# w_out converted from 64 to 32 bits during the attention, through a scratch in DRAM

## The chip, the cores and the metric

The kernel runs on one core of one Trainium2 chip. The metric is the device time of one execution in microseconds (us), lower is better. Beside the time there is a profile of one execution, with the start and the duration of each instruction on each engine: TensorE (PE, with its weight loads as PEld), VectorE (DVE), ScalarE (ACT), GpSimd (POOL), and SyncE (SP), which here only issues DMAs.

## The reference

Three stages follow one another. B = 4, H = 8 heads, 512 local and 32 global positions, head size 64, so 2304 tokens of 512 channels.

```python
# 1 attention: global rows see everything, local rows the global ones and a window of 32
out_g = softmax(scale * q_g @ k_all.T) @ v_all
out_l = softmax([scale * q_l @ k_g.T, where(|i - j| <= 32, scale * q_l @ k_l.T, -1e9)]) @ [v_g, v_l]
x = concat([out_g, out_l]).transpose(0, 2, 1, 3).reshape(2304, 512)
# 2 mixture of 8 experts, 288 tokens each, assigned greedily by descending logit
logits = x @ w_gate
for e in range(8):
    out[mask_e] = relu(x[mask_e] @ w1[e]) @ w2[e]         # 512 -> 1024 -> 512
# 3 feed-forward for all tokens
h = out @ w_in                                            # 512 -> 2048
result = (max(h, 0) + log1p(exp(-abs(h)))) @ w_out        # 2048 -> 512
```

The two weights of the third stage, `w_in` (512 x 2048) and `w_out` (2048 x 512), come with 64 bits per number; all other inputs have 32.

## The kernel before

**Numbers.** The products of the experts' stages are made in three passes: each 32-bit operand is split into a high part in the engine's 32-bit matmul format and the rest, and TensorE adds high x high, high x rest and rest x high (`mm3`). A split is one copy (high part, on ScalarE or GpSimd) and one subtraction (rest, on GpSimd through `psub`, or on VectorE). A 64-bit weight must first be made into a 32-bit one, by shifts and masks on its two 32-bit halves.

**Attention** (`attention`, lines 115 to 197) runs in 64 steps of software pipelining, eight to a unit (a pair of batch and half of the heads), and some steps after. A letter of `CFG["order"]` stands for a piece of a step: scores on TensorE (`a`), maximum on VectorE (`m`), exponent on ScalarE (`e`), transposes (`c`), products with V (`d`), normalizing (`n`), logits (`p`), the next unit's K and Q transposes (`u`) and V windows (`v`), the loads of the units to come (`q`, `w`), and the global rows (`g`). Results go to `xs_scratch` in DRAM, the global rows last; these are read back (`xg`) for their logits, the last that the routing waits for (`global_finish`, `lastly`).

**w_in** is converted during the attention. Pieces `k` and `b` call `conv_a(n)` and `conv_b(n)` (lines 260 to 286), for 16 blocks of 128 x 512 numbers. `conv_a` loads a 64-bit block of 512 KB on SP's queue into one of three buffers. `conv_b`, four steps later, takes magnitude and sign (L277 and L278, ScalarE), and a step after that shifts and joins bits (L281, L282, VectorE), multiplies by the sign (L283, which the profile shows as the helper's L255, GpSimd), and stores 256 KB to `win_scratch` (L284, SP's queue). One block goes every three steps, from step 6 on (`"k": 6, "r": 3`). After the attention `load_win` reads the sixteen 32-bit tiles of w_in back, and `conv_win` splits them: copy on ScalarE (L589), subtraction on GpSimd (L258).

**w_out** is loaded as it is, in 64 bits: ten blocks of 512 KB at step 58 (`EARLY`), when the attention's first buffers are given up, and six more after the last store to `xs_scratch`. `conv_wout` (lines 597 to 617) is the conversion in four steps: magnitude on ScalarE (L606), three bit operations on VectorE (L608, L610, L612), then the split, copy on ScalarE (L616) and subtraction on GpSimd (L258).

**After the attention.** `route(0, hop)` finds the tokens of the first expert, by two searches of three levels; at each level VectorE compares (L686, L687), TensorE counts, and VectorE decides. `hop` is called after each comparison but the first and puts steps of `conv_wout` there, by the costs `COST` and the allowance `HOP`. Then the tokens' rows are gathered (`gather`, GpSimd's indirect DMA), transposed and split (`xh`, `xl`). For each expert `moe1` runs the two products of stage 2 over eight blocks `f`, and `moe2` the two of stage 3 over sixteen; the next expert's routing is spread over both. In the first expert `conv` is called with each block and puts there what is left of w_out's steps and the last five of w_in's splits (`NW`, `C0`, `CS`); also, its w1 and w2 blocks are split otherwise than later ones (high part on ScalarE, rest of seven of the w2 blocks on GpSimd).

**Order.** Each engine runs its instructions in its own queue's order. That order is made when the program is built, by a planner that simulates the program's time, with additional edges from `after`, which places the instructions of an engine behind a given instruction of the same engine. DMAs of the kernel are issued on SP's queue, in order, but for the gathers and the final stores (GpSimd).

Of the kernel before, what the change touches and what calls it, by code (L numbers as in the profile page):

```python
# [8 lines left out]
F32 = mybir.dt.float32  # L9
# [10 lines left out]
P = 128  # L20
# [22 lines left out]
CFG = {"order": "adcm*wnpvbehuqkgDxA", "c": 1, "d": 2, "n": 5, "x": 5, "p": 6, "u": 0, "w": 2, "g": [3, 4, 7], "g7": [0, 1, 3], "b": 4, "ps": [1, 2, 2, 3], "pp": 2, "ph": 2, "nb": 2, "xc": 4, "qs": 1, "cv": 3, "k": 6, "r": 3, "m": 0, "e": 0, "h": 1, "z": 4, "uA": 0, "uD": 0, "gD": 0, "gA": 0, "hA": 1, "hD": 1, "nD": 1, "xA": 0, "pD": 1, "cD": 1, "v": [2, 3, 4, 5, 6, 7], "ve": "DPPPPP", "ue": "ADAaaDA", "he": "A", "ge": "DDA"}  # L43
COST = (0.335, 0.6, 0.6, 0.0)
HOP = {64: 1.2, 32: 0.7}
NEARLY = 10
MC = {"MT0": [0, 1, 3, 5, 10, 11, 12, 14, 15, 17, 20, 21, 24, 25, 26], "MT1": [1, 2, 3, 4, 5, 7, 12, 13, 14, 15, 16, 17, 18, 20, 23], "GT": [24, 1], "GW": 10, "AH": 1, "XB": 8, "HEAD": 4, "L2": "bkadc", "lag": {"a": 0, "b": 1, "c": 2, "d": 3}, "bufs": {"sp_e": 3, "sp_u": 3, "gh": 3, "gl": 4, "wh": 4, "wl": 4, "wraw": 4}, "HT0": "ABhhh", "HT1": "Ahhh", "C0": 6, "CS": 0.75, "NW": 11, "NWT": 3, "WH": "PPPA", "WL": "DDDD", "M1L": 2, "H1": 0, "OB": "ADB", "W0": "PPPPPPPD"}
# [8 lines left out]
class K:  # L56
    def __init__(self, tc, ctx, a):
        self.tc = tc
        self.nc = tc.nc
        self.ctx = ctx  # L60
        self.a = a
        self.xs = self.nc.dram_tensor("xs_scratch", (NTOK, D), F32).ap()
        self.wic = self.nc.dram_tensor("win_scratch", (D, DFF), F32).ap()

# [46 lines left out]
    def attention(self):  # L111
# [27 lines left out]
        for s in range(6):  # L139
# [19 lines left out]
            "k": lambda t, u, s, live: (t - G["k"]) % G["r"] == 0 and 0 <= (t - G["k"]) // G["r"] < 16 and self.conv_a((t - G["k"]) // G["r"]),  # L159
            "b": lambda t, u, s, live: (t - G["k"] - G["b"]) % G["r"] == 0 and 0 <= (t - G["k"] - G["b"]) // G["r"] < 16 and self.conv_b((t - G["k"] - G["b"]) // G["r"]),  # L160
# [38 lines left out]
    def half(self, t, fn):  # L199
        if t >= 0 and t % 2 == 0 and t < 64:  # L200
            fn(t // 2)

# [57 lines left out]
    def conv_a(self, n):  # L260
        nc, ap = self.nc, self.ap
        w = 512
        q, cc = n // 4, n % 4
        src = self.a["moe2_w_in"].bitcast(I32)[cc * P:cc * P + P, q * 2 * w:(q + 1) * 2 * w]
        dst = self.wic[cc * P:cc * P + P, q * w:q * w + w]
# [320 lines left out]
    def conv_win(self, f):  # L586
        w = self.wi[f]
        rv = w[:, 1].bitcast(F32)
        self.nc.scalar.copy(w[:, 0], rv)  # L589
        self.psub(w[:, 1], rv, w[:, 0].bitcast(F32))  # L590
# [6 lines left out]
    def conv_wout(self, f):  # L597
        nc, mp = self.nc, self.mp
        rv = self.wo[f].rearrange("p (n t) -> p n t", t=2)
        lo, hi = rv[:, :, 0], rv[:, :, 1]  # L600
        if self.late:
            m, u = (mp.tile([P, D], I32, tag=n, bufs=MC["bufs"][n], name=f"wou{n}{f}") for n in ("wh", "wl"))
        else:
            mu = mp.tile([P, 2, D], I32, tag=("yL", "yh", "yl")[f % 3], bufs=1, name=f"wou{f}")
            m, u = mu[:, 0], mu[:, 1]
        nc.scalar.activation(m.bitcast(F32), hi.bitcast(F32), AF.Abs, scale=2.0 ** -112)  # L606
        yield
        nc.vector.tensor_scalar(u, lo, 29, None, ALU.logical_shift_right)  # L608
        yield
        nc.vector.scalar_tensor_tensor(u, hi, -(2 ** 31), u, ALU.bitwise_and, ALU.bitwise_or)  # L610
        yield
        nc.vector.scalar_tensor_tensor(u, m, 3, u, ALU.logical_shift_left, ALU.bitwise_or)  # L612
        yield
        w = u.bitcast(F32)
        self.wo[f] = o = self.wop.tile([P, 2, D], F32R, tag=f"wo{f}", bufs=1, name=f"wo{f}")
        nc.scalar.copy(o[:, 0], w)  # L616
        self.psub(o[:, 1], w, o[:, 0].bitcast(F32))
# [414 lines left out]
    def moe(self):  # L1032
        self.moe_setup()
# [6 lines left out]
        self.late = False  # L1040
        gens = [self.conv_wout(f) for f in range(16)]
        todo = [(f, i) for f in range(16) for i in range(4)]

        def step():
            f, i = todo.pop(0)
            if i == 0:
                next(gens[f])
            next(gens[f], None)
            return COST[i]
# [11 lines left out]
        with self.after(self.r_ins):  # L1061
            for f in range(MC["NW"]):
                self.conv_win(f)
# [87 lines left out]
```

## Time and profile before

| what | value |
|---|---|
| median of 3 runs | 907.5 us (902.51 to 910.68) |
| the profiled execution | span 906.8 us from its first to its last instruction; no other time is given for it |
| granted TensorE clock, mean | 0.946 |
| busy: PE, PEld | 819.0 us (90%), 717.3 us (79%) |
| busy: DVE, ACT, POOL | 673.6 us (74%), 428.0 us (47%), 453.7 us (50%) |
| DMA | 87.36 MB, mean 96 GB/s |
| chain of waits | PE 64%, DVE 25%, DMA 4%, issue 3%, POOL 2% |

"Busy" is the time in which an engine shows at least one instruction; matmuls are pipelined, so a busy PE need not be at its peak. The chain of waits is followed back from the last instruction, at each step to what released it. The granted clock is the share of full speed that TensorE was given. An instruction carries the line of the kernel that issued it, and a copy or a subtraction through a helper that of the helper (L82 `pcopy`, L255 `pmul`, L258 `psub`). The shares of the whole span are averages over stages with different limits.

### The profile page before, as it was taken

Reading aid. Unit: us, or ns where it says so; the run is one execution under the profiler, and the core shown is the slowest. Engines: PE = TensorE matmul, PEld = TensorE weight load, DVE = VectorE, ACT = ScalarE, POOL = GpSimd, SP = SyncE. Lnnn points to the kernel's source line nnn. Section 1 sums busy time; section 2 is a strip of 40 time slices with the busy share of each in tenths; the row PEclk is TensorE's granted clock in tenths of the full one; section 3 lists DMA queues with packets and bytes.
Section 4 is the critical chain, followed back from the end, with each engine's and each line's share of the span. In section 5 each row is a group of like instructions: output and inputs, shape, how many; then the busy total and the mean of one; then the engine's idle time right before and its main releaser. Section 6 shows DMA issues by size and latency. Waiting matters only on the chain.

```text
span 906.8 us, 20945 instructions
## 1 busy us (share of the span) xinstructions
PE 819.0 (90%) x7608; PEld 717.3 (79%) x7608; DVE 673.6 (74%) x1981; ACT 428.0 (47%) x1067; POOL 453.7 (50%) x608
## 2 busy tenths in 40 slices
PE   7999999931488989999999999999999999999996
PEld 4677767621478869989978998998899899889885
DVE  4776877579999887786795887679588778763632
ACT  3667767532554552453345255244525524442542
POOL 6654758034767554464366265336435643642533
PEclk9999999955588999999999999999999999999999
DMA  6879773792230124122131321303132130312000
GB/s 150 193 208 248 212 202 121 267 311 77 71 94 1 55 64 117 47 72 86 33 94 44 99 70 49 109 10 97 45 95 84 36 117 2 118 59 60 1 1 35
DMA packets 123691, 87.36 MB, mean 96 GB/s; under 512 B 61828, under 2 KB 106884, under 8 KB 123588
## 3 DMA queue, kind: packets, MB, share of 16 engines
q1 hardware_dynamic: 120692, 77.11, 30.0%
q0 software_dynamic: 2896, 8.92, 3.0%
q8 instruction: 60, 0.98, 0.5%
q14 instruction: 43, 0.35, 0.1%
HBM read 72.89 MB, written 13.11 MB: 95 GB/s over the span
## 4 chain that ended last, share of the span: by engine, by line
PE 64%; DVE 25%; DMA 4%; issue 3%; POOL 2%; ACT 1%; SPq 1%; POOLq 0%; ACTq 0%; DVEq 0%
PE accb L1008 12%; PE h L884 8%; PE h L886 8%; PE h L885 8%; PE st L399 4%; PE acca L884 3%; PE acca L885 3%; PE acca L886 3%; DVE sp_e L990 3%; DVE R L811 2%; PE av L447 2%; PE pt L429 2%; DVE gl L999 2%; DVE wl L879 2%; DMA wr<-in_moe_w_dram 1%
## 5 line engine op out<-in xcount | busy, mean ns | idle before, releaser
L1008 PE MATMUL accb<-wo,gh 128*128 128x512 f32 x448 | 131.9, 400 | 1.0 <-ACT gh L998 1.0
L997 POOL TENSOR_TENSOR sp_u<-sp_u,sp_e 128x256 f32<-128x256 f32 x112 | 89.9, 806 | 83.4 <-DVE sp_e L991 33.3
L884 PE MATMUL h<-yh,wi 128*128 128x256 f32 x448 | 127.7, 291 | 0.8 <-DVE yl L943 0.8
L885 PE MATMUL h<-yl,wi 128*128 128x256 f32 x448 | 128.1, 288 | 0.0
L886 PE MATMUL h<-yh,wi 128*128 128x256 f32 x448 | 127.9, 288 | 0.0
L879 DVE TENSOR_TENSOR wl<-wr,wh 128x512 fp32r<-128x512 f32 x121 | 92.5, 778 | 12.8 <-POOL wh L82 9.8
L82 POOL TENSOR_SCALAR wh<-wr 128x512 fp32r<-128x512 f32 x84 | 60.1, 720 | 82.7 <-PE h L885 50.5
L990 DVE SCALAR_TENSOR_TENSOR sp_e<-sp_u,sp_e 128x256 f32<-128x256 f32 x112 | 59.4, 531 | 43.2 <-POOL sp_u L985 43.2
L884 PEld LDWEIGHTS h<-yh,wi 128*128 128x128 f32 x448 | 86.8, 196 | 4.6 <-DVE yl L943 1.0
L886 PEld LDWEIGHTS h<-yh,wi 128*128 128x128 f32 x448 | 87.8, 196 | 3.1
L885 PEld LDWEIGHTS h<-yl,wi 128*128 128x128 f32 x448 | 87.8, 196 | 2.9
L1008 PEld LDWEIGHTS accb<-wo,gh 128*128 128x128 f32 x448 | 77.1, 189 | 12.6 <-ACT gh L998 1.8
L985 POOL TENSOR_SCALAR sp_u<-sp_e 128x256 f32<-128x256 f32 x112 | 64.0, 576 | 44.5 <-ACT sp_e L984 34.0
L886 PE MATMUL h<-xh,wl 128*128 128x272 f32 x256 | 76.4, 299 | 9.2 <-DVE wl L879 9.1
L1008 PE MATMUL accb<-wo,gl 128*128 128x512 f32 x224 | 79.2, 402 | 3.8 <-DVE gl L999 3.7
L992 ACT ACTIVATE sp_u<-sp_u 128x256 f32<-128x256 f32 x112 | 46.7, 417 | 66.8 <-DVE sp_e L990 66.2
L884 PE MATMUL h<-xh,wh 128*128 128x272 f32 x256 | 77.2, 302 | 0.9 <-ACT xh L867 0.9
L885 PE MATMUL h<-xl,wh 128*128 128x272 f32 x256 | 75.4, 295 | 0.0
L885 PE MATMUL acca<-hl,wh 128*128 128x272 f32 x256 | 71.3, 293 | 2.2 <-DVE hl L920 2.2
L919 ACT ACTIVATE hh<-h 128x272 fp32r<-128x272 f32 x64 | 25.4, 396 | 97.7 <-PE h L886 89.3
L886 PE MATMUL acca<-hh,wl 128*128 128x272 f32 x256 | 70.9, 291 | 0.0
L983 ACT ACTIVATE sp_e<-h 128x256 f32<-128x256 f32 (+1 forms) x128 | 49.0, 387 | 43.2 <-PE h L886 43.2
(410 smaller groups left out, 2212.5 us busy)
## 6 DMA issues: line engine op xcount, KB each, us to landing
wr<-in_moe_w_dram SPq DMA_DIRECT2D x128, 256.0 KB, 2.8
wraw<-in_moe_w_in_dram SPq DMA_DIRECT2D x16, 512.0 KB, 5.0
wor<-in_moe_w_out_dram SPq DMA_DIRECT2D x16, 512.0 KB, 7.1
qn<-in_q_l_dram SPq DMA_DIRECT2D x32, 128.0 KB, 2.9
xs_scratch<-xc SPq DMA_DIRECT2D x32, 128.0 KB, 3.9
win_scratch<-cvs SPq DMA_DIRECT2D x16, 256.0 KB, 4.3
wi<-win_scratch SPq DMA_DIRECT2D x16, 256.0 KB, 5.7
kn<-in_k_l_dram SPq DMA_DIRECT2D x40, 96.0 KB, 3.8
```

Of the source, the lines that this page charges most:

```text
L82: self.nc.gpsimd.tensor_scalar(out, in_, 1.0, 1.0, ALU.mult, ALU.mult)
L399: nc.tensor.matmul(o, q[:, pr, i].rearrange("p r q -> p (r q)"), kw, start=True, stop=True)
L879: (nc.gpsimd if (odd and MC["W0"][self.wn // 2 % 8] == "P" if first else MC["WL"][self.wn % 4] == "P") else nc.vector).tensor_tensor(l, ra ...
L884: nc.tensor.matmul(ps, wh, ah, start=start, stop=False)
L885: nc.tensor.matmul(ps, wh, al, start=False, stop=False)
L886: nc.tensor.matmul(ps, wl, ah, start=False, stop=stop)
L983: nc.scalar.activation(e, ps, AF.Abs)
L985: nc.gpsimd.tensor_scalar(u, e, 1.0, 1.0, ALU.add, ALU.mult)
L990: nc.vector.scalar_tensor_tensor(e, u, -1.0, e, ALU.add, ALU.subtract)
L992: nc.scalar.activation(u, u, AF.Ln)
L997: nc.gpsimd.tensor_tensor(u, u, e, ALU.add)
L1008: nc.tensor.matmul(t, g[:, cs], w, start=f == 0 and i == 0, stop=f == 15 and i == 2)
```

## The change

w_out goes the way that w_in goes. `conv_a` and `conv_b` now run for 32 blocks, first 16 of w_out (128 whole rows each, 512 KB in, 256 KB out to the new `wout_scratch`), then the 16 of w_in. They are spread by `spread`: block n at step 1 + floor(15 n / 8), the last at step 59, `conv_b` still four steps later. `load_wout` reads 32-bit blocks of 256 KB, at the same two places. `conv_wout` and `conv_win` go; `split` does a tile's copy (ScalarE) and subtraction (VectorE or GpSimd). The list `todo` has eight w_out tiles, the sixteen of w_in, and the other eight of w_out: `hop` takes two after a comparison with 64 thresholds and one after one with 32, on VectorE; `conv` takes two per block in the first eight blocks of expert 0, the first on GpSimd and the second on VectorE, and then one per block on GpSimd, until none is left. The diff without the tables' unchanged entries and the two `conv_*` functions that go:

```diff
-CFG = {... "k": 6, "r": 3, ...}
-COST = (0.335, 0.6, 0.6, 0.0)
-HOP = {64: 1.2, 32: 0.7}
+CFG = {... "k": 1, "r": 15, ...}
-MC = {... "C0": 6, "CS": 0.75, "NW": 11, "NWT": 3, ...}
+MC = {...}
@@ __init__
+        self.woc = self.nc.dram_tensor("wout_scratch", (DFF, D), F32).ap()
@@ attention
-            "k": lambda t, u, s, live: (t - G["k"]) % G["r"] == 0 and 0 <= (t - G["k"]) // G["r"] < 16 and self.conv_a((t - G["k"]) // G["r"]),
-            "b": lambda t, u, s, live: (t - G["k"] - G["b"]) % G["r"] == 0 and 0 <= (t - G["k"] - G["b"]) // G["r"] < 16 and self.conv_b((t - G["k"] - G["b"]) // G["r"]),
+            "k": lambda t, u, s, live: self.spread(t - G["k"], self.conv_a),
+            "b": lambda t, u, s, live: self.spread(t - G["k"] - G["b"], self.conv_b),
+    def spread(self, t, fn):
+        for n in range(2 * DFF // P):
+            if n * CFG["r"] // 8 == t:
+                fn(n)
@@ conv_a
-        q, cc = n // 4, n % 4
-        src = self.a["moe2_w_in"].bitcast(I32)[cc * P:cc * P + P, q * 2 * w:(q + 1) * 2 * w]
-        dst = self.wic[cc * P:cc * P + P, q * w:q * w + w]
+        if n < 16:
+            src = self.a["moe2_w_out"].bitcast(I32)[n * P:n * P + P]
+            dst = self.woc[n * P:n * P + P]
+        else:
+            q, cc = (n - 16) // 4, n % 4
+            src = self.a["moe2_w_in"].bitcast(I32)[cc * P:cc * P + P, q * 2 * w:(q + 1) * 2 * w]
+            dst = self.wic[cc * P:cc * P + P, q * w:q * w + w]
@@ load_wout
-        raw = self.wop.tile([P, 2 * D], I32, tag=f"wo{f}", bufs=1, name=f"wor{f}")
-        self.wo.append(raw)
-        self.nc.sync.dma_start(raw, self.a["moe2_w_out"].bitcast(I32)[f * P:f * P + P])
+        o = self.wop.tile([P, 2, D], F32R, tag=f"wo{f}", bufs=1, name=f"wo{f}")
+        self.wo.append(o)
+        self.nc.sync.dma_start(o[:, 1].bitcast(F32), self.woc[f * P:f * P + P])
+    def split(self, item, eng):
+        kind, f = item
+        w = self.wo[f] if kind == "o" else self.wi[f]
+        r = w[:, 1].bitcast(F32)
+        self.nc.scalar.copy(w[:, 0], r)
+        eng.tensor_tensor(w[:, 1], r, w[:, 0].bitcast(F32), ALU.subtract)
@@ moe
+        todo = [("o", f) for f in range(8)] + [("i", f) for f in range(16)] + [("o", f) for f in range(8, 16)]
         def hop(ins, n):
-            left = HOP[n]
             with self.after(ins):
-                while left > COST[todo[0][1]]:
-                    left -= step()
-                if todo[0][1] == 3:
-                    step()
+                for _ in range(n // 32):
+                    self.split(todo.pop(0), nc.vector)
...
-        with self.after(self.r_ins):
-            for f in range(MC["NW"]):
-                self.conv_win(f)
...
             with self.after(*(self.x_ins if t else first)):
-                w = MC["NW"] + t - MC["NWT"]
-                if t >= MC["NWT"] and w < 16:
-                    self.conv_win(w)
-                n = 4 * max(MC["C0"] + MC["CS"] * t, t - 5 if t > 7 else 0)
-                while todo and (64 - len(todo) < n or todo[0][1]):
-                    step()
+                for e in "PD" if t < 8 else "P":
+                    if todo:
+                        self.split(todo.pop(0), nc.gpsimd if e == "P" else nc.vector)
```

## Rows read from the trace of the kernel before

**Rows 1.** The page's slices (fortieths of the span): DMA busy tenths, and GB/s.

```profile
DMA  6879773792230124122131321303132130312000
GB/s 150 193 208 248 212 202 121 267 311 77 71 94 1 55 64 117 47 72 86 33 94 44 99 70 49 109 10 97 45 95 84 36 117 2 118 59 60 1 1 35
```

**Rows 2.** Busy us of each engine, summed over six attention units, 33.1 to 162.4 us.

```profile
sum 129.30, PE 126.36 PEld 91.64 DVE 98.84 ACT 91.16 POOL 80.79; mean PE 21.06 PEld 15.27 DVE 16.47 ACT 15.19 POOL 13.47
```

**Rows 3.** Chain of waits, 11 to 164 us: shares of the stretch by engine and line.

```profile
by line: PE st L399 22.7%; PE av L447 11.0%; PE pt L429 10.8%; PE kps L343 6.1%; PE sg L507 6.0%; PE pl L477 5.5%; DVE cvt L281 4.9%; PE xt L467 4.8%; PE avg L544 4.4%; PE qps L370 4.0%; PE pga L531 3.1%; issue 2.8%; DVE cvt L282 2.3%; DVE 
```

**Rows 4.** Chain of waits, 172 to 189 us: start us, us, what.

```profile
172.27 7.16 DMA xs_scratch<-gs
179.45 6.05 DMA xg<-xs_scratch
```

**Rows 5.** Timeline of VectorE at the tail: start us, us, engine, line, operation.

```profile
183.28 0.17 DVE L478 TENSOR_SCALAR L<-pl 128x8 f32<-128x8 f32 x1 [1.66 <-PE pl L477]
188.61 0.17 DVE L478 TENSOR_SCALAR L<-plg 128x8 f32<-128x8 f32 x1 [3.85 <-PE plg L477]
```

**Rows 6.** Busy us by stretch: route, two halves of expert 0, two of expert 1.

```profile
core 0: us, PE busy (x) PEld busy (x) DVE busy (x) ACT busy (x) POOL busy (x), PEclk, DMA share, GB/s
188.60:225.90 37.30, 6.53 (x121) 4.97 (x118) 35.22 (x105) 10.68 (x19) 17.38 (x13) 0.50 0.63 177
235.30:284.20 48.90, 35.41 (x263) 32.72 (x263) 47.95 (x81) 27.19 (x51) 32.86 (x26) 0.81 0.15 44
284.20:336.30 52.10, 48.12 (x346) 42.53 (x346) 43.77 (x129) 26.22 (x67) 32.05 (x43) 0.95 0.18 52
338.40:368.10 29.70, 29.70 (x293) 28.91 (x292) 22.38 (x62) 6.98 (x17) 10.53 (x17) 1.00 0.31 90
368.10:414.70 46.60, 44.94 (x308) 40.03 (x307) 37.47 (x110) 25.66 (x67) 26.79 (x40) 1.00 0.20 58
```

**Rows 7.** Groups by line and shape, 0 to 164 us: the conversion's instructions.

```profile
L255 POOL TENSOR_TENSOR cvs<-cvt,cvs 128x512 f32<-128x512 f32 x16 | 21.0, 1317 | 16.3 <-ACT cvs L278 5.3 <-issue 2.1 <-DVE rc L456 2.1
L282 DVE SCALAR_TENSOR_TENSOR cvt<-cvm,cvt 128x512 int32<-128x512 int32 x16 | 15.5, 969 | 0.2
L281 DVE TENSOR_SCALAR cvt<-wraw 128x512 int32<-128x512 int32 x16 | 14.4, 899 | 0.1
L278 ACT ACTIVATE cvs<-wraw 128x512 f32<-128x512 f32 x16 | 10.9, 684 | 0.0
```

**Rows 8.** The tile cvt: duration ns min/median/max, first and last start.

```profile
L281 DVE TENSOR_SCALAR cvt<-wraw x16: 411/604/2722, 38.0 to 146.7; 128x512 int32<-128x512 int32 x16
L282 DVE SCALAR_TENSOR_TENSOR cvt<-cvm,cvt x16: 677/692/1798, 39.5 to 147.9; 128x512 int32<-128x512 int32 x16
```

**Rows 9.** Timeline of VectorE in the route for expert 0.

```profile
193.08 0.23 DVE L700 TENSOR_SCALAR xk<-xk,base0h 128x17 f32<-128x17 f32 x1
195.50 1.27 DVE L700 TENSOR_SCALAR xk<-xk,base0h 128x17 f32<-128x17 f32 x1
215.89 1.32 DVE L760 SCALAR_TENSOR_TENSOR G<-xk,base0l,A 128x136 bf16<-128x136 f32 x1
217.14 0.35 DVE L761 SCALAR_TENSOR_TENSOR G<-xk,base0l,A 128x136 bf16<-128x136 f32 x1
```

**Rows 10.** Busy us on tiles wou, then wouwl: DVE, ACT, POOL, by stretch.

```profile
188.60:225.90 37.30, 4.55 (x6) 2.61 (x5) 2.53 (x2) 0.50 0.63 177
235.30:284.20 48.90, 18.65 (x21) 9.33 (x15) 14.44 (x10) 0.81 0.15 44
...
235.30:284.20 48.90, 6.29 (x9) 1.24 (x2) 1.57 (x2) 0.81 0.15 44
```

**Rows 11.** Groups by line and shape, VectorE, 235.3 to 284.2 us.

```profile
L879 DVE TENSOR_TENSOR wl<-wr,wh 128x512 fp32r<-128x512 f32 x7 | 7.5, 1075 | 0.0
```

**Rows 12.** Chain of waits in expert 0, TensorE at two clocks.

```profile
249.74 0.23 PE h L884
267.90 0.13 PE h L884
```

More of the change, by code (lines that the diff above doesn't have):

```diff
@@ L42 @@
 EARLYC = 12
[L43 to L45 removed]
+CFG = {"order": "adcm*wnpvbehuqkgDxA", "c": 1, "d": 2, "n": 5, "x": 5, "p": 6, "u": 0, "w": 2, "g": [3, 4, 7], "g7": [0, 1, 3], "b": 4, "ps": [1, 2, 2, 3], "pp": 2, "ph": 2, "nb": 2, "xc": 4, "qs": 1, "cv": 3, "k": 1, "r": 15, "m": 0, "e": 0, "h": 1, "z": 4, "uA": 0, "uD": 0, "gD": 0, "gA": 0, "hA": 1, "hD": 1, "nD": 1, "xA": 0, "pD": 1, "cD": 1, "v": [2, 3, 4, 5, 6, 7], "ve": "DPPPPP", "ue": "ADAaaDA", "he": "A", "ge": "DDA"}
 NEARLY = 10
[L47 removed]
+MC = {"MT0": [0, 1, 3, 5, 10, 11, 12, 14, 15, 17, 20, 21, 24, 25, 26], "MT1": [1, 2, 3, 4, 5, 7, 12, 13, 14, 15, 16, 17, 18, 20, 23], "GT": [24, 1], "GW": 10, "AH": 1, "XB": 8, "HEAD": 4, "L2": "bkadc", "lag": {"a": 0, "b": 1, "c": 2, "d": 3}, "bufs": {"sp_e": 3, "sp_u": 3, "gh": 3, "gl": 4, "wh": 4, "wl": 4, "wraw": 4}, "HT0": "ABhhh", "HT1": "Ahhh", "WH": "PPPA", "WL": "DDDD", "M1L": 2, "H1": 0, "OB": "ADB", "W0": "PPPPPPPD"}
 LEFT = CAP - 2 * P
@@ L584, in load_win @@
         nc.sync.dma_start(w[:, 1].bitcast(F32), self.wic[:, f * P:f * P + P].rearrange("(c p) k -> p c k", p=P))
[L586 to L590, printed above, removed]
-    def load_wout(self, f):
-        raw = self.wop.tile([P, 2 * D], I32, tag=f"wo{f}", bufs=1, name=f"wor{f}")
-        self.wo.append(raw)
-        self.nc.sync.dma_start(raw, self.a["moe2_w_out"].bitcast(I32)[f * P:f * P + P])
[L597 to L617, printed above, removed]
+    def load_wout(self, f):
+        o = self.wop.tile([P, 2, D], F32R, tag=f"wo{f}", bufs=1, name=f"wo{f}")
[7 more added lines that the diff above has]
+        eng.tensor_tensor(w[:, 1], r, w[:, 0].bitcast(F32), ALU.subtract)
     def wtile(self, t):
@@ L1032, in moe @@
     def moe(self):
+        nc = self.nc
         self.moe_setup()
@@ L1039, in moe @@
                 self.load_wout(f)
[L1040 to L1049, printed above, removed]
+        todo = [("o", f) for f in range(8)] + [("i", f) for f in range(16)] + [("o", f) for f in range(8, 16)]
         def hop(ins, n):
-            left = HOP[n]
             with self.after(ins):
-                while left > COST[todo[0][1]]:
-                    left -= step()
-                if todo[0][1] == 3:
-                    step()
+                for _ in range(n // 32):
+                    self.split(todo.pop(0), nc.vector)
         for _ in self.route(0, hop):
             pass
-        with self.after(self.r_ins):
-            for f in range(MC["NW"]):
-                self.conv_win(f)
         g = self.gather(0)
@@ L1112, in hook2 @@
                 tick(f + 8)
-            self.late = True
             self.moe2(k, y, hook2)
```

## The prediction

> **What bounds the kernel now.** I read the page's slices first, then stretches of the trace in time order: attention (0 to 164 us), its tail to 188.6, routing for the first expert to 225.9, the first expert to 336.3, and a later expert for comparison. From the second expert on nothing of the change runs any more; those 560 us I leave alone. The slices show how heavily DMA is used during the attention: six to nine tenths in all but the last of its seven [rows 1].
>
> In six inner units of the attention TensorE shows as busy for 126.4 of 129.3 us, VectorE for 98.8, ScalarE for 91.2 and GpSimd for 80.8 [rows 2]. The chain of waits says the same: mostly matmul lines, but the two VectorE steps of the weight conversion stand in it with 4.9% and 2.3% of 153 us, 11.0 us for 16 conversions, 0.69 us each [rows 3]. So attention is TensorE's, with VectorE close behind.
>
> The tail is a matter of DMA. The last global rows take 7.16 us to be written and 6.05 us to be read back [rows 4], beside ten loads of 512 KB w_out blocks. The last ordinary logits were ready at 183.28, the global ones at 188.61 [rows 5].
>
> Routing and the first expert are VectorE's: busy 35.2 of 37.3 us in the route and 47.95 of 48.9 us in the first half of the first expert [rows 6]. The same two halves of the next expert take 29.7 and 46.6 us; of the first, 48.9 and 52.1 [rows 6]. The first expert is thus 24.7 us longer than the next, 19.2 of it in its first half.
>
> **The change, part by part.**
>
> Attention, 16 more conversions. Each issues two DMAs on SP's queue (0.5 MB in, 0.25 MB out), two ScalarE instructions of about 0.68 us, two of VectorE (0.90 + 0.97 us on average) and one GpSimd multiplication of 1.32 us [rows 7]. None touches TensorE. If VectorE were the whole bound, 16 x 1.87 = 30 us; if they go as the present ones do in the chain, 16 x 0.69 = 11 us. Below that I see no reason to go: this is added work and nothing leaves the attention. I take the shortest the pair is seen at, 0.41 + 0.68 = 1.09 us [rows 8], times 16: **+17 us**. It lies between, as VectorE, 76% busy in the six units, has gaps but not all of them usable. ScalarE's 16 x 1.36 = 22 us and GpSimd's 21 us run beside that. DMA: 12.6 MB more, at the 311 GB/s of the fullest slice some 40 us of transfer; the slices of the attention show 0.6 to 0.9 busy [rows 1], so about 115 of 163 us become 155: nearly full, still not the bound. On SP's queue 32 more issues go past the K, Q, V loads and the stores of finished rows. Reads come every 1.9 steps instead of every 3, with three buffers that are each held five steps, so a read now waits whenever VectorE is late by over half a step, and the next unit's loads stand behind it. Those loads are issued more than one unit ahead for K and Q; V has the least cover. That is why my upper end is the full 30.
>
> Tail. The first ten loads shrink from 5.2 to 2.6 MB. The global rows then land sooner, and what is late next is the last ordinary block, 5.3 us earlier than now [rows 5]. Against it, the last conversions now run to the end of the attention and use the same DMA. **-4 us**, bounds -5 and 0.
>
> Route for expert 0. Now 13 GpSimd subtractions, 17.4 us, run in it [rows 6]; eleven are w_in splits (NW in MC), which the change moves behind the route, and its own first GpSimd split waits for the gather. While GpSimd runs, VectorE's small instructions are long: the same line takes 0.23 us at 193.08, before GpSimd starts, and 1.27 us at 195.50; two alike take 1.32 and 0.35 us at 215.89 and 217.14, the first under a subtraction [rows 9]. From 195.50 to 215.89 ten routing steps are stretched so, by 11 us in sum against their short twins. The Trainium skill, SBUF — State Buffer (Who interferes with whom), says that VectorE and GpSimd share a port pair as an exclusive lock, held for a whole instruction, the second to issue blocking fully. By that rule up to all 17.4 us of GpSimd's work could have blocked VectorE, and the sum would be 888 us; the rows show 11 us, and I go by them. In between the routing's searches six w_out steps of VectorE (4.6 us [rows 10]) give way to six subtractions, 512 columns with two inputs like the bit step that takes 0.68 us at its shortest [rows 8]: 4.1 us, no difference that I count. **-11 us**, bounds -12 and -5 (the searches wait for counts in between, so part of a shortening may turn into waiting).
>
> First expert, first half. The w_out steps hold VectorE for 18.65 + 6.29 = 24.9 us of it [rows 10]. In their place stand seven subtractions of 512 columns, which in this stretch take 1.08 us [rows 11]: 7.5 us. VectorE's need falls from 47.95 to 30.5 us, about the 29.7 us that the next expert takes. ScalarE, busy for 27.2 us [rows 6], loses 10.6 us of w_out steps and gains 14 copies of 0.62 us (9.33 / 15 [rows 10]); GpSimd's 32.9 us become about 24 (seven w2 subtractions and seven splits at 14.44 / 10 us [rows 10], and some 4 us of small copies of y). Neither exceeds 30.5. TensorE starts at half clock (granted 0.50 in the route [rows 6]), its instructions 0.23 us apart instead of 0.13 [rows 12]; at half clock (1.2 GHz) throughout, 192 instructions x 0.23 = 44 us. Between 30.5 and 44 I take 36: the clock in this stretch already averages 0.81 although VectorE leaves TensorE idle for 13 us of it [rows 6], so it will be mostly full. **-13 us**, bounds -19 (as the next expert) and -5 (44).
>
> First expert, second half. It loses the last w_out steps at its head (part of its 5.5 us over the next expert) and gets ten GpSimd splits of 1.4 us that stood earlier. GpSimd would have 26.8 (the next expert's [rows 6]) + 14 = 41 of 46.6 us, with its sum of the activation queued behind each split. **-2 us**, bounds -5 and +3. Between route and first expert (9.4 us) nothing is counted: the gather and its transposes set its end.
>
> Sum: 17 - 4 - 11 - 13 - 2 = -13 us on the profiled execution's 906.8 us, 893.8; the median of the runs, 907.5, is 0.7 above it: **894 us**. All best ends together give -30 (877), all worst +23 (930).
>
> **The rivals.**
>
> Slower: VectorE and GpSimd hinder each other in the attention as they do in the route. Every added conversion brings its 1.32 us multiplication there, and the pair of VectorE's own conversion steps is seen at 1.09 us undisturbed but 1.87 on average [rows 7, 8], so VectorE is already held up. If multiplication and conversion steps exclude each other in full and VectorE finds no gap, the price is 3.19 us each, 51 us, and with 30 gained elsewhere the time is 907.5 + 21 = 928. It decides from 1.9 us per added conversion; above 2.4 the kernel is slower by over 1%. Against it: VectorE is idle for 30 of 129 us [rows 2], and the present conversions, with the same multiplication, put 0.69 us each on the chain [rows 3]. Chance 0.13. The Trainium skill's rule of the exclusive lock (SBUF — State Buffer, Who interferes with whom) speaks for this rival: it names VectorE instructions with two SBUF inputs against GpSimd ones that read SBUF, and a conversion brings one of each.
>
> No change, by the attention: it grows by the full 30 us and gives back everything: about 907. For it speak the almost full DMA and SP's queue, against it the chain's 0.69. Chance 0.13.
>
> No change, by the clock: the first expert's first half stays at half clock, 44 us: gain 5 instead of 13, 902. For it speaks the low clock during the route, which the change leaves as sparse as it is; against it the 0.81 granted now. Chance 0.12.
>
> More gained: the conversions hide as the present ones do (+11) and the first expert runs like the next: 877 to 885. Chance 0.12.
>
> That the change does not do what it says I give nothing: w_out's 48 bit steps on VectorE cannot stay where their instructions are no longer issued.
>
> **How the numbers follow.** The forecast, 886 to 899, has 0.50. A difference under 1% (9 us) cannot be told from none. Faster: the forecast and "more gained", 0.62. Within 1%: both "no change" cases, 0.25. Slower: 0.13. The range leaves out the slower case and takes in the others, with 7 us above 907 for an attention that costs a little more than VectorE's full 30: 877 to 914.
>
> **What would show it.** Route from the global logits to the first expert's indices near 26 us instead of 37, with GpSimd empty in it; first half of expert 0 near 36 us and VectorE no longer busy throughout; attention's end, seen at the last logits, 183 now, near 200. If the last logits come after 215, the attention term is wrong and the time will not fall; if the route stays at 37 us with GpSimd empty, the port was not the cause of the long steps; if expert 0 stays at 49 us, VectorE was not its bound.

## The result, and the profile after

The changed kernel takes **917.32 us** (median of 12 runs, 913.29 to 922.64) against 908.26 (902.51 to 913.54, 12 runs) for the kernel before on the same chips: ratio 1.010, 95% interval 1.0071 to 1.0129. It is 1% slower; the forecast was 894, and 917.3 lies 3 us above its range of 877 to 914. The profiled execution has a span of 913.8 us, 3.5 under the median, 7.0 over the span before.

Stages by their marks in the two timelines (last ordinary logits, global logits, first expert's indices, its first matmul, last `yl` of `moe1`, last `xl` for expert 1; us). [rows 6] ends the first half at the first `yl`, 1 us earlier; each column is one profiled execution:

| stage | before | after | difference | forecast |
|---|---|---|---|---|
| attention, to the last ordinary logits | 183.3 | 201.8 | +18.5 | +17 |
| tail, to the global logits | 5.3 | 6.9 | +1.6 | -4 |
| route for expert 0 | 37.2 | 25.4 | -11.8 | -11 |
| gather | 9.4 | 9.0 | -0.4 | 0 |
| expert 0, first half | 50.0 | 49.7 | -0.3 | -13 |
| expert 0, second half | 53.2 | 49.0 | -4.2 | -2 |
| the other seven | 568.4 | 572.0 | +3.6 | 0 |

The last row runs the same instructions in both; over all the runs below it lies between 568.1 and 573.2 us, and I read nothing from it.

Page of the changed kernel: the slices, which answer to [rows 1]. Of the seven slices up to 160 us, four now stand at eight or nine tenths (two before), and the seventh rose from three to seven.

```profile
DMA  6998877698302213121130312303132130312000
GB/s 145 220 244 230 226 213 231 203 336 246 117 13 82 69 50 117 34 85 61 57 93 25 116 49 70 92 26 93 39 103 69 51 107 11 107 64 64 1 1 34
```

Windows of the changed kernel, by attention unit (the sum answers to [rows 2]), then route, two halves of expert 0 and two of expert 1 (to [rows 6]); columns as there:

```profile
core 0: us, PE busy (x) PEld busy (x) DVE busy (x) ACT busy (x) POOL busy (x), PEclk, DMA share, GB/s
33.40:54.90 21.50, 19.25 (x306) 13.74 (x310) 17.72 (x71) 15.55 (x43) 14.51 (x17) 1.00 0.89 244
...
143.10:173.10 30.00, 26.61 (x407) 18.14 (x402) 23.83 (x88) 21.52 (x54) 21.02 (x20) 1.00 0.59 191
sum 139.70, PE 126.71 PEld 90.90 DVE 103.81 ACT 98.55 POOL 86.98; mean PE 21.12 PEld 15.15 DVE 17.30 ACT 16.43 POOL 14.50
...
173.10:193.10 20.00, 17.47 (x249) 12.29 (x250) 15.01 (x61) 17.17 (x43) 6.63 (x5) 0.74 0.99 348
...
208.60:234.00 25.40, 6.49 (x122) 5.00 (x119) 23.34 (x104) 1.31 (x3) 0.00 (x0) 0.50 0.74 217
243.00:292.70 49.70, 34.64 (x284) 32.88 (x285) 38.72 (x69) 25.40 (x49) 33.47 (x28) 0.77 0.17 49
292.70:341.80 49.10, 46.92 (x332) 41.96 (x331) 39.24 (x118) 26.44 (x68) 25.01 (x41) 0.97 0.19 55
341.80:371.00 29.20, 29.20 (x274) 27.89 (x274) 22.87 (x59) 5.97 (x14) 9.38 (x12) 1.00 0.30 91
371.00:420.80 49.80, 48.00 (x334) 43.03 (x333) 40.25 (x115) 27.83 (x73) 28.44 (x46) 0.97 0.18 55
```

The six units took 129.3 us and now take 139.7 with the same busy time of TensorE (126.4 and 126.7): it waits more. A unit is counted from one maximum over its scores to the same one of the next unit. Of the 18.5 us, 14.2 are in the last two units, 30.0 and 20.0 us (22.4 and 13.4 before). Asked for evenly, the conversions don't stand evenly: units 1 to 5 hold 16 of them, where the kernel before had 14, and took 109.7 us against 106.9; units 6 and 7 hold twelve, where it had two, and three more stand behind. The route has GpSimd at 0.00 and is as short as forecast. The first half of expert 0 has VectorE no longer full (38.7 of 49.7) and is no shorter. Its timeline, changed kernel (TensorE, ScalarE, GpSimd, VectorE; in brackets the idle time before a group and what ended it):

```profile
243.03 1.16 PE L871 MATMUL h<-xh,wh 128*128 128x272 f32 x2 [0.30 <-ACT xh L854]
253.43 0.60 PE L871 MATMUL h<-xh,wh 128*128 128x272 f32 x1 [4.41 <-ACT wh L862]
264.86 0.60 PE L873 MATMUL h<-xh,wl 128*128 128x272 f32 x1 [9.71 <-DVE wl L866]
...
242.88 8.42 ACT L603 CAST wi<-wi 128x512 fp32r<-128x512 f32 x16
251.20 1.66 ACT L603 CAST wo<-wo 128x512 fp32r<-128x512 f32 x3
252.75 0.62 ACT L862 CAST wh<-wr 128x512 fp32r<-128x512 f32 x1
...
243.58 13.39 POOL L604 TENSOR_TENSOR wi<-wi 128x512 fp32r<-128x512 f32 x9 [1.55 <-ACT wi L603]
256.93 9.01 POOL L604 TENSOR_TENSOR wo<-wo 128x512 fp32r<-128x512 f32 x5
...
248.01 1.25 DVE L721 TENSOR_TENSOR sgn<-sgn,M 128x17 int32<-128x17 int32 x1
258.04 5.10 DVE L604 TENSOR_TENSOR wi<-wi 128x512 fp32r<-128x512 f32 x3
263.06 1.75 DVE L866 TENSOR_TENSOR wl<-wr,wh 128x512 fp32r<-128x512 f32 x1
```

The splits are asked for two per block in the program, but they depend on nothing of a block, and the planner has put them in one run at the head of the half: 19 copies on ScalarE ahead of the block's `wh`, 14 subtractions in a row on GpSimd, and VectorE's instructions stretched beside them (17 numbers a partition in 1.25 us). TensorE waits 4.4 and 9.7 us for the high part and the rest (`wh`, `wl`) of the block's own weights. All 24 splits that route and gather left over, 17 of them on GpSimd (26.1 us), run in this half.

The tail, changed kernel, chain of waits and VectorE's timeline (to [rows 4, 5]): the read of the global rows takes 8.26 us instead of 6.05.

```profile
197.28 8.26 DMA xg<-xs_scratch
```

```profile
201.80 0.17 DVE L486 TENSOR_SCALAR L<-pl 128x8 f32<-128x8 f32 x1
208.65 0.17 DVE L486 TENSOR_SCALAR L<-plg 128x8 f32<-128x8 f32 x1 [2.90 <-PE plg L485]
```

### The profile page after: what moved, and what is told of

Read it like the earlier page. It is cut to its first block, busy times and chain, and to the rows that moved or that the text cites. A ratio compares the mean times of both kernels' runs of the same rounds, so it can differ in the third digit from the quotient of the medians.

```text
span 913.8 us, 21064 instructions
## 1 busy us (share of the span) xinstructions
PE 825.2 (90%) x7608; PEld 721.6 (79%) x7608; DVE 658.0 (72%) x1979; ACT 437.1 (48%) x1083; POOL 447.3 (49%) x610
## 4 chain that ended last, share of the span: by engine, by line
PE 64%; DVE 22%; DMA 4%; issue 4%; POOL 2%; ACT 2%; SPq 1%; POOLq 0%; ACTq 0%; DVEq 0%
PE accb L995 12%; PE h L871 8%; PE h L873 8%; PE h L872 8%; PE st L407 5%; PE acca L873 3%; PE acca L871 3%; PE acca L872 3%; DVE sp_e L977 3%; PE pt L437 2%; DVE R L798 2%; PE av L455 2%; DVE gl L986 2%; DMA wr<-in_moe_w_dram 2%; DVE wl L866 1%
## 5 line engine op out<-in xcount | busy, mean ns | idle before, releaser
L977 DVE SCALAR_TENSOR_TENSOR sp_e<-sp_u,sp_e 128x256 f32<-128x256 f32 x112 | 55.6, 497 | 41.8 <-POOL sp_u L972 41.8
L972 POOL TENSOR_SCALAR sp_u<-sp_e 128x256 f32<-128x256 f32 x112 | 61.9, 557 | 47.3 <-ACT sp_e L971 32.7
L906 ACT ACTIVATE hh<-h 128x272 fp32r<-128x272 f32 x64 | 25.4, 397 | 100.3 <-PE h L873 91.9
```

Of the source, the lines that this page charges most:

```text
L972: nc.gpsimd.tensor_scalar(u, e, 1.0, 1.0, ALU.add, ALU.mult)
L977: nc.vector.scalar_tensor_tensor(e, u, -1.0, e, ALU.add, ALU.subtract)
```

## Experiments

All are compared with the kernel before on the same chip: time (median), then the ratio with its 95% interval. "Theory" and "rival" are those written down before each run.

### Expert 0: the splits' places

**Paced splits** (changed kernel; `pace` is the block before's ReLU copy, its rest `hl` and a weight's rest; in `moe2` the exponent and GpSimd's sum):

```diff
-            with self.after(*(self.x_ins if t else first)):
+            with self.after(*(self.pace if t else first)):
```

> The changed kernel, with each block's splits in the first expert put behind the block before (behind its ReLU on ScalarE, its rest on VectorE, its subtraction on GpSimd) instead of only behind the gathered rows; the same work. Theory: the first half of the first expert takes 48 us (243.0 to 291.5) because all 16 w_in copies stand in one run on ScalarE at 242.9 and 14 subtractions in one run on GpSimd at 243.6, ahead of w1's and w2's splits, so that TensorE is idle for 9.7 + 4.4 us and falls to half clock. Paced, it takes 33 to 38 us and the time falls by 10 to 15 us, to 902 to 907. Rival: the sum of the work on VectorE, GpSimd and ScalarE holds it, or the half clock that the route leaves behind; then it stays at 44 to 48 us and the time at 913 to 918.

920.31 us, ratio 1.0129 (1.0065 to 1.0193). The first half fell to 37.1 us, as the theory said, but the second rose to 64.3, and the theory's 902 to 907 in all failed. Windows, paced kernel: in the second half GpSimd is busy for 40.6 us (25.0 in the changed kernel) and VectorE for 54.3 (39.2): the next expert's routing now runs there beside one split per block.

```profile
243.90:281.00 37.10, 31.60 (x272) 29.42 (x272) 33.67 (x65) 20.05 (x39) 20.56 (x15) 0.89 0.25 72
281.00:345.30 64.30, 52.38 (x368) 44.61 (x369) 54.28 (x135) 31.34 (x80) 40.55 (x55) 0.95 0.14 42
```

So the order explains the missing 13 us. Pacing alone gives it back, since what was done during the stall now falls into the second half.

**The kernel before, its w_in splits later** (`"NW": 11, "NWT": 3` to `0, 0`: none in the route, one per block from the first on).

> The kernel before, with all 16 w_in splits put into the first expert, one for each of its blocks, instead of eleven in the route. Theory (GpSimd's subtractions stretch VectorE in the route): the route from the global logits to the first indices takes 25 to 27 us instead of 37.2, as in the changed kernel (25.4), though w_out's bit steps stay in it; the two subtractions of w_out that stay cost 1 to 2 of that. The first expert gets longer by 0 to 8 us, and the time falls by 3 to 10 us, to 898 to 905. Rival (the route became shorter since w_out's bit steps left it): it stays at 35 to 37 us and the time is 908 or more.

910.9 us, 1.0028 (1.0002 to 1.0053). The route fell to 27.0 us (37.2), and the first half of expert 0 rose to 62.7 (50.0). So the splits lengthen the route, whatever w_out does. That it is GpSimd's part of them, and not ScalarE's copies, a later run shows: with copies in the route (ScalarE busy for 8.0 us) and GpSimd at 0.00 it took 25.4. But what leaves the route lands on the first half, VectorE busy 62.2 of 62.7 us.

**Splits in the gather's gap**: twelve while the gathered rows are on their way, GpSimd and VectorE in turn, twelve paced one per block.

```diff
-                for e in "PD" if t < 8 else "P":
+                for e in "PD" * 6 if t == 0 else "PD"[t % 2]:
```

First with the attention of the run with five buffers (below), then with the changed kernel's:

> The kernel of the spread conversions with expert 0's splits placed otherwise: six on GpSimd and six on VectorE in the 9 us between the token indices and the first matmul of expert 0, where the changed kernel had three, and the other twelve one per block, each behind the activations and the subtraction of the block before, on the two engines in turn. Theory (the first half of expert 0 waits because the splits stand in one run ahead of its own instructions on ScalarE, GpSimd and VectorE, and pacing alone gave it back in the second half because VectorE and GpSimd are full there): first half 37 to 41 us, second half 49 to 53, together 87 to 93 instead of 98.7, and the time 6 to 11 us under that of the spread conversions alone. Rival (the splits in the gap delay the gathered rows' own transposes, copies and rests, which need the same three engines): the gap grows from 9 to 12 us or more, both halves together stay at 95 or more, and the time is within 3 us of the spread conversions alone.

Unclear: its four runs took 916.49, 929.6, 931.1 and 931.48 us, too far apart to set against that attention's own 934.59. In the trace, of the 931.48 us run, the gather took 9.0 us and the halves 36.1 and 53.1.

> The changed kernel, its attention untouched, with expert 0's splits placed as in the kernel with the spread conversions and the gap: six on GpSimd and six on VectorE in the 9 us between the token indices and the first matmul, the other twelve one per block behind the block before. There the first half fell to 36.1 us, the second rose to 53.1, without a longer gap. Theory (the first half's stall is the run of splits ahead of its own instructions, and what the gap takes off the engines is not given back): first half 36 to 38, second 49 to 53, together 87 to 90 instead of 98.7, and the time 906 to 911, 7 to 11 us under the changed kernel. Rival (given back, as by pacing alone): both halves together 96 to 101 and 915 to 920.

910.16 us, 1.0018 (0.9993 to 1.0042), 7 us under the changed kernel. The time is the theory's. First half 31.8, second 54.0, but the gap grew from 9.0 to 15.7, as the rival of the run just above had it. Gap and halves together took 101.5 us against 107.7: using the gap was worth 6 us. Why it grew, VectorE and GpSimd in the timeline of that kernel:

```profile
235.99 3.09 DVE L604 TENSOR_TENSOR wi<-wi 128x512 fp32r<-128x512 f32 x5
239.00 11.25 DVE L866 TENSOR_TENSOR wl<-wr,wh 128x512 fp32r<-128x512 f32 x2
...
239.89 1.28 POOL L604 TENSOR_TENSOR wo<-wo 128x512 fp32r<-128x512 f32 x1
241.11 6.15 POOL L604 TENSOR_TENSOR wi<-wi 128x512 fp32r<-128x512 f32 x5
247.23 2.47 POOL L866 TENSOR_TENSOR wl<-wr,wh 128x512 fp32r<-128x512 f32 x2
```

One VectorE subtraction took 0.73 us, its twin 10.60, until the run of eight GpSimd subtractions beside it was over.

**The same in the kernel before** (eleven w_in splits from the route to the gap).

> The kernel before (w_out converted in expert 0 and the routing), with one edit: the eleven splits of w_in that stood in the routing stand in the gap between the token indices and the first matmul, six on GpSimd and five on VectorE, the other five one per block as before. Theory (the routing is long because GpSimd splits there: 27.0 us without it; and what made the first half of expert 0 longer by 12.7 us when these splits came later was that they stood on GpSimd ahead of its own work, which the gap takes away in good part): routing 26 to 28, first half 48 to 54, and 895 to 902 in all. Rival (VectorE, which must still do the bit steps of 14 blocks of w_out behind the routing, is the limit of the first half whatever GpSimd does): first half 58 to 63 and 906 to 911.

917.78 us, 1.0104 (1.0058 to 1.0149). Theory and rival both failed: the route was 27.1, as the theory said, but the gap became 24.5 us, with 16 GpSimd instructions (19.7 us) and VectorE busy throughout on splits and bit steps, and the first half stayed at 55.2. In these two kernels, the gap was worth something only where w_out's bit steps are gone.

### Attention: which part of a conversion costs

**w_out's DMAs alone** (nothing converted; other numbers stored):

```diff
+        if n < 16:
+            return self.defer("D", CFG["cD"], lambda: nc.sync.dma_start(dst, self.fill))
```

> The changed kernel, in which the 16 w_out blocks of the attention are loaded and stored (the store takes a constant tile) but not converted: no instruction of ScalarE, VectorE or GpSimd for them; w_out's values are other ones. The attention's last ordinary logits came at 183.3 before and 201.8 after. Theory (the engines' work makes the attention longer): they come at 183 to 189, and the time falls by 12 to 18 us to 899 to 905. Rival (transfers and SP's queue): they stay at 195 to 202, and the time at 911 to 918.

914.39 us, 1.0061 (1.0031 to 1.0092), last logits at 203.0, as late as with all the work. But all of w_in's conversions stand in units 5 to 7 and behind here, so this run does not part the DMAs from that pile-up.

**The work alone** (one loaded block converted 16 times, one stored; w_out's tiles then come from w_in's scratch).

> The changed kernel, in which the 16 w_out blocks are converted from one block that is loaded once, and only the first is stored: the engines' work without the transfers (12.6 MB less 0.8); w_out's tiles are then read from w_in's scratch, so its values are other ones. Theory (the engines' work makes the attention longer): the last ordinary logits come at 197 to 202, as in the changed kernel; with the tail less crowded the time is 911 to 917. Rival (transfers and SP's queue): they come at 184 to 190, and the time is 900 to 906. If both this and the kernel without the conversion's instructions come near 192, each carries a half.

920.69 us, 1.0114 (1.0045 to 1.0183), last logits at 213.9. Not a clean test: without loads to wait for, the planner bunched w_out's conversions in the first three units (units 1 and 2: 37.1 and 29.4 us, 17.3 and 26.7 before; VectorE 88% and 81% busy).

**Five buffers and earlier conversions** (`"cv": 3` to 5, `"r": 15` to 12).

> The changed kernel with five conversion buffers instead of three, and the 32 conversions asked for every 1.5 steps instead of every 1.875; in the order that results the last conversion stands in the middle of unit 7 and no unit holds more than 7, where the changed kernel had 12 in units 6 and 7 and three behind the last unit. Theory (the attention pays for the pile-up at its end: units 6 and 7 took 50.0 us, against 35.8 before): those two units fall to 38 to 44 us, the last ordinary logits come at 190 to 196 instead of 201.8, the global logits at 195 to 201 instead of 208.6, and the time is 906 to 911. Rival (the sum of the work counts, wherever it stands: 16 more conversions at about 1 us of the engines that bound the attention): the other units lengthen by what these two lose, the last logits stay at 199 to 204 and the time at 914 to 920.

934.59 us, 1.0298 (1.0248 to 1.0348), last logits at 226.2. The theory of the pile-up fell: with eight conversions instead of twelve, units 6 and 7 still took 49.0 us, and units 2 to 5 109.3 instead of 88.2.

**No conversion of w_out** (tiles from w_in's scratch).

> The changed kernel without any conversion of w_out: only w_in is converted during the attention, at the steps at which the kernel before did it, and the experts' w_out tiles are loaded from w_in's scratch (so the second product uses other numbers). Everything behind the attention is as in the changed kernel. Theory (the whole loss is the attention's and the tail's; the stages behind the global logits gave 16 us): last ordinary logits at 183 to 186, global logits at 187 to 190, then 25.4 us of routing and about 99 us for expert 0, and 893 to 898 us in all. Rival (the stages behind don't give 16 us when the attention ends early, because their gain was a wait that the late attention had covered, such as the loads of the split tiles): routing over 30 us or expert 0 over 105 us, and 903 to 908 in all.

897.37 us, 0.9869 (0.9814 to 0.9924). Route 25.5, expert 0 98.3: what lies behind the attention gives its 16 us wherever the attention ends. The last logits came at 191.0, later than the theory's 183 to 186; units 0 to 6 were those of before to 0.1 us, and in the last unit eight of ScalarE's copies for the splits now stand (4.8 us). The changed kernel has them there too (181.0 to 195.1 us), so some 5 us of its 18.5 may be these; no run shows it.

**GpSimd out of the conversion** (sign by a third VectorE operation, no ScalarE Sign):

```diff
+            nc.vector.scalar_tensor_tensor(u, hi, -(2 ** 31), u, ALU.bitwise_and, ALU.bitwise_or)
-            self.pmul(sg, u.bitcast(F32), sg)
```

> The changed kernel with GpSimd taken out of the conversion: the sign is put on by a third VectorE operation (the sign bit of the upper half or'ed in) instead of ScalarE's Sign and GpSimd's multiplication; 32 multiplications of 1.27 us on GpSimd and 32 Signs of 0.67 us on ScalarE less, 32 operations of 0.7 to 0.9 us on VectorE more. The kernel before had in the changed one's attention half as many multiplications. Theory (the attention is lengthened by the mutual hindrance of the two: while a GpSimd multiplication runs, VectorE's instructions that take nothing from PSUM stretch, as 0.24 to 1.2 us at 166.3 to 170 us, and TensorE waits for the VectorE instruction behind them, 2.94 us at 173.25): the last ordinary logits come at 188 to 196 instead of 201.8 and the time is 904 to 911. Rival (VectorE's sum of work is what lengthens the attention: 16 x 2 operations more than before, and 32 more in this run): last logits at 204 to 220 and 920 to 935. Between the two: neither engine decides alone.

925.33 us, 1.0195 (1.0164 to 1.0225), last logits at 207.4. My theory fell here too: 32 more VectorE operations, with 32 of ScalarE's and 32 of GpSimd's less, cost 8 us by the medians. With the gap's splits added:

> Both of the edits of the two runs before it: GpSimd out of the conversion, and the splits in the gap. If they are independent, its time is the changed kernel's plus both differences; by the theories 917 - 10 - 9, so 896 to 902, under the kernel before. By the rivals 920 or more.

913.0 us, 1.0052 (1.0025 to 1.0079): 12 under the run above it, 3 over the gap alone, between what theory and rival gave.

**One part of w_out's conversions left out at a time**: first their DMAs alone again, with w_in's conversions at the steps where they were before; then everything but VectorE's operations; then everything but Sign and multiplication. w_in's blocks are converted in full in all three.

> As the earlier run with w_out's DMAs alone (each block loaded and a block of other numbers stored, nothing converted), but w_in's conversions stand about where the kernel before has them (one per three steps, the last at step 53), with load buffers of their own for w_out. The earlier run had them in the last four units, four to six a unit, and its last logits at 203.0. Theory (VectorE's operations are the price, and there it was w_in's bunch): last ordinary logits at 183 to 190 and 895 to 903 in all. Rival (the 32 more DMAs on SP's queue and the 6.3 MB delay the loads of q, k and v): last logits at 196 to 203 and 908 to 916.

> The changed kernel without VectorE's two operations for w_out's 16 blocks: they are loaded, ScalarE's two and GpSimd's multiplication run, and the product is stored (w_out's numbers are other ones then); w_in's blocks are converted in full. Theory (VectorE's operations are the price, 1.1 us a block and more where they stretch): last logits at 184 to 192, 898 to 906 in all. Rival (GpSimd's multiplications or the DMAs are): last logits at 198 to 205 and 912 to 919.

> The changed kernel without ScalarE's Sign and GpSimd's multiplication for w_out's 16 blocks (all its numbers come out positive); VectorE's two operations and the DMAs run as in the changed kernel. Theory (VectorE's operations are the price, wherever GpSimd is): last logits at 197 to 203, 911 to 918 in all. Rival (GpSimd's multiplication holds VectorE up, 16 more of 1.27 us): last logits at 184 to 193 and 899 to 907.

| | time us | ratio | last logits |
|---|---|---|---|
| DMAs alone | 917.47 | 1.0106 (1.0067 to 1.0145) | 209.4 |
| without VectorE's | 909.05 | 0.9995 (0.9968 to 1.0023) | 201.1 |
| without Sign and product | 919.54 | 1.0103 (1.0059 to 1.0146) | 203.9 |

Leaving out Sign and GpSimd's multiplication gains nothing, as the theory of VectorE's price had it. But leaving out VectorE's operations gains only 8 us by the medians (0.7 in the last logits of the profiled executions), of the 20 between the changed kernel and the one without w_out's conversion, and with the DMAs alone the kernel is as late as with everything. The parts don't add up: each alone is late enough.

Two things limit these readings. Kernels with the same attention differ, too: the last logits came at 181.3, 183.3 and 184.6 us with the old one and at 201.8, 203.8 and 205.8 with the changed one, so 4 us between two traces show nothing. And what w_in's twelve conversions in units 6 and 7 cost, where the changed kernel lost 14.2 of its 18.5 us, no run of this kind shows: they stay there in the last two, and those units took 52.4 and 50.5 us (50.0 in the changed kernel). Windows of units 5, 6 and 7, DMAs alone and, below, the kernel before:

```profile
121.20:141.80 20.60, 16.11 (x204) 10.78 (x201) 12.21 (x53) 14.04 (x39) 10.88 (x12) 0.92 0.97 299
141.80:183.50 41.70, 36.01 (x464) 25.80 (x464) 24.57 (x93) 20.98 (x51) 21.95 (x19) 0.67 0.73 220
183.50:199.70 16.20, 14.21 (x220) 10.20 (x220) 7.64 (x45) 12.44 (x36) 0.00 (x0) 0.89 0.59 193
```

```profile
117.10:140.00 22.90, 21.66 (x344) 15.48 (x343) 16.87 (x69) 15.01 (x42) 12.44 (x13) 0.93 0.76 225
140.00:162.40 22.40, 22.18 (x405) 16.45 (x402) 19.45 (x81) 17.05 (x46) 14.94 (x14) 1.00 0.26 82
162.40:175.80 13.40, 12.40 (x217) 9.19 (x218) 7.76 (x47) 8.09 (x26) 0.00 (x0) 1.00 0.95 352
```

DMA share and GB/s are the last two columns. Before, the DMA engines had caught up by unit 6 (0.26); with 32 more transfers they run full through unit 5 (0.97), the V loads for unit 7 are issued at 155 to 163 us (136 to 145 before), and in unit 6 VectorE, ScalarE and GpSimd are idle for four to five tenths, TensorE at 0.67 of its clock. In the changed kernel itself it is less plain. Its unit 6 lost 7.6 us with the DMA engines at 0.59; in unit 7, with them at 0.99, the chain of waits has ScalarE's next Sign wait for the store of a converted block:

```profile
174.33 5.27 DMA win_scratch<-cvs
```

**w_out last.** w_in where it was before, w_out behind it, into units 5 to 7; four buffers:

```diff
-        for n in range(2 * DFF // P):
-            if n * CFG["r"] // 8 == t:
-                fn(n)
+        for n in range(16):
+            if 3 * n == t:
+                fn(n + 16)
+            if 28 + n * CFG["r"] // 8 == t:    # k 6, r 14, cv 4
+                fn(n)
```

> The changed kernel with the blocks' order turned round: w_in's 16 are asked for where the kernel before had them (one per three steps from step 6) and w_out's 16 behind them, one per 1.75 steps from step 34 on, with four buffers instead of three. All the work is the same, but units 1 to 4 hold only what they held before, and w_out's DMAs fall into units 5 to 7. Theory (the attention pays for DMAs added to units whose DMA engines were 0.76 to 0.94 busy): units 0 to 5 as before (126 us), units 6 and 7 together 40 to 48 us, last ordinary logits at 191 to 197, and 906 to 912 in all. Rival (what counts is how much is added, and a pile-up at the end costs as much): last logits at 200 to 206 and 915 to 921.

906.86 us, 0.9993 (0.9975 to 1.0011): 10.5 under the changed kernel with the same work. Last logits at 189.9, just ahead of what the theory gave; units 0 to 5 took 121.9 us, units 6 and 7 44.1. The tail took 8.4. Windows of units 5, 6 and 7:

```profile
113.60:135.30 21.70, 20.92 (x355) 15.05 (x351) 16.90 (x67) 16.78 (x47) 13.21 (x14) 1.00 0.90 244
135.30:160.80 25.50, 23.06 (x373) 16.17 (x372) 22.78 (x81) 17.55 (x45) 20.28 (x18) 1.00 0.77 234
160.80:179.40 18.60, 16.14 (x246) 11.17 (x246) 18.09 (x65) 16.03 (x42) 8.20 (x6) 0.72 0.83 297
```

Eleven conversions stand in units 6 and 7 here, nearly as many as the twelve of the changed kernel, so a pile-up there need not cost what it cost that one. The fourth buffer was not tried by itself; the run with five buffers was the slowest of all. With the splits in the gap:

> The same with expert 0's splits in the gap, which took 7 us off the changed kernel. Theory: 899 to 905, under both the kernel before and the changed one. Rival: 908 to 914.

**897.13 us, 0.9879** (0.9832 to 0.9926): under both, and 2 us under what the theory gave. Windows of that kernel (route, two halves of expert 0):

```profile
198.50:224.90 26.40, 6.43 (x120) 4.91 (x117) 24.34 (x106) 8.03 (x13) 1.26 (x1) 0.50 0.91 263
233.60:270.60 37.00, 32.17 (x284) 31.34 (x285) 31.12 (x63) 16.85 (x33) 20.34 (x21) 0.86 0.24 72
270.60:324.40 53.80, 49.87 (x343) 42.86 (x343) 45.59 (x123) 29.18 (x75) 31.27 (x44) 0.97 0.16 51
```

## Why the prediction was wrong

**The step that failed: expert 0's first half, -13 us forecast, -0.3 measured.** "VectorE's need falls from 47.95 to 30.5 us" priced sums of work and took the splits to stand two per block, as the program asks for them. `after` ties them to nothing later than `x_ins`, so the planner put them first, and all 17 of GpSimd's, of which I had put ten into the second half, ran in the first. VectorE's busy time fell only to 38.7, TensorE idled for 14 us (4.4 and 9.7) until the block's own halves were made, and VectorE's instructions were stretched beside GpSimd's run. Paced, the half took 37.1 us, near my 36; but that gain was then lost in the second half (64.3), which I had priced alone and not with the work that a shorter first half hands on. The clock was no cause of its own: granted 0.77 in that half with the stalls, 0.86 and 0.89 in the two paced kernels shown.

**Second half: -2 forecast, -4.2 measured, by luck.** The ten GpSimd splits that I had added to it had already run in the first half; none stands in it.

**Tail: -4 forecast, +1.6 measured.** The loads shrank, but two loads and five stores of the last conversions are now issued behind the last unit, and the read of the global rows took 2.2 us longer. Where conversions end earlier (five buffers) or w_out's are left out (no conversion, DMAs alone) the tail is 1.7 us, which fits; no run moved these transfers alone. I had named the counter-effect and sized it too small.

**Attention: +17 forecast, +18.5 measured; the size is right by luck.** I charged VectorE's pair of operations, 1.09 us a block, and called the DMA "nearly full, still not the bound". Without that pair for w_out's blocks the last logits came 0.7 us earlier and the median fell by 8. With the DMAs alone they came as late as with everything, and with the same work but w_out's blocks behind w_in's (and a fourth buffer) 11.9 us earlier. So the transfers and the order of the blocks count for more than VectorE's sum of work. What held the changed kernel itself stays open: most of its loss is in units 6 and 7, where w_in's conversions pile up, the DMA engines are full only in the second of these, and every run has an order of its own. The engines' work isn't free either, as the work alone and GpSimd's share put on VectorE show. Whether it is the DMA engines' time or SP's one queue that counts, no run parts.

**Route: -11 forecast, -11.8 measured**, by the mechanism named; the two runs that moved only w_in's splits in the kernel before show it apart from the change (27.0, 27.1).

**The rivals.** "No change, by the attention" (907) and "slower" (928) lie about equally far from 917, with 30 and 51 us for the attention, which took 18.5. The first named DMA and SP's queue. For the second, GpSimd's multiplication, nothing speaks: without w_out's 16 the time was 919.54, without all 32 (VectorE doing the work) 925.33. "No change, by the clock" is out too.

Sum of the stages: 18.5 + 1.6 - 11.8 - 0.4 - 0.3 - 4.2 + 3.6 = +7.0 us.

## What to carry to other kernels

Before moving transfers into a stage, look at the DMA share unit by unit and put them where it is low; a mean of 0.75 hid units at 0.94 and one at 0.26, and moving w_out's blocks behind w_in's, with a fourth buffer, was worth 10.5 us here, though what held the attention is shown only in part. Work that depends on nothing stands where the planner puts it, so price a stage by the order its queue will have, and tie such work to the stage's own progress. And when a stall goes, cost the next stage again with what it now receives.

## What was not expected of the hardware

A VectorE subtraction of 128x512 with both inputs in SBUF took 10.60 us, against 0.73 for its twin, until eight GpSimd subtractions issued back to back (9.9 us) were done. The Trainium skill, SBUF — State Buffer (Who interferes with whom), has the two block each other for a whole instruction; here the wait went through a whole run of instructions. In the last kernel above a VectorE operation of 128x136 took 5.94 us in the same way, beside seven GpSimd subtractions. It is not always so: in the changed kernel three VectorE subtractions took 5.10 us in all beside five of GpSimd in a row (9.01 us). What decides between the two no run shows.

The DMA page of the kernel before, 13 to 176 us:

```profile
DMA packets 59240, 33.37 MB, mean 205 GB/s; under 512 B 50505, under 2 KB 53961, under 8 KB 59207
```

Most packets are the rows of Q, K and V, and 0.75 of the DMA engines' time moved 205 GB/s; in the last unit, with the 64-bit blocks of w_out, 0.95 moved 352. The Trainium skill, DMA: Bandwidth & Descriptors (Specifications), gives 512 bytes as the least transfer for full rate; the trace agrees: 50505 of the 59240 packets above are smaller, and 264 of the 1399 in the last unit. Bytes therefore told me less than the busy share.
